# Attention scores of the second pair of heads: three float32r products of split operands in place of one float32 product

## The chip, the cores and the metric

The kernel runs on one core of one Trainium2 chip. The metric is the device time of one execution in microseconds; three runs gave 1058.92, 1059.16 and 1059.59, median 1059.16 us. A core has TensorE (PE; its weight loads are shown as PEld), VectorE (DVE), ScalarE (ACT), GpSimd (POOL) and SyncE (SP), which here issues nearly all DMA transfers. PSUM, the memory that TensorE writes, has eight banks of 2 KB a partition; SBUF holds the rest of the on-chip data in 128 partitions.

## The reference

Inputs are q, k and v of shape 8 x 12 x 448 x 64 (batches, heads, positions, width of a head), two weight matrices of 768 x 2048 and 2048 x 768, and two scalars. All is float32.

```python
scores = scale * np.matmul(q, k.transpose(0, 1, 3, 2)) - np.log(S)
attn = 1.0 / (1.0 + np.exp(-scores))
attn_out = np.matmul(attn, v)
x = attn_out.transpose(0, 2, 1, 3).reshape(B * S, H * D)     # 3584 x 768
h = x @ w_in
g = s * np.maximum(h, 0.0) ** 2 + b
out = g @ w_out
```

The sigmoid takes the place of a softmax, so there is no row sum: each score goes through scale, bias and sigmoid by itself, and the result multiplies v. Then comes a feed-forward block over all 3584 tokens.

## The kernel before

The program is laid out by hand: the order in which instructions are written is the order of each engine's queue, and a tile of memory that is used again makes its next writer wait for the last readers.

**Attention stage.** 24 steps ("quads", line 333), three to a batch, each of four heads. The four heads are two pairs: index i is the pair, index j the head within it. The two heads of a pair lie in partitions 0 to 63 and 64 to 127 of the tiles `q` and `k` (`half`, line 332). `scores` (L357) goes over the pairs and over three blocks c of 128 keys; for each it computes two float32 products of 64 contraction rows, one for each head, into a PSUM tile of two banks (L365), and ACT turns both at once into weights by a sigmoid (L354). The last 64 keys of all four heads go together in 64x64 tiles (`scores_last`, L372, products L377); this is written for step n+1 behind the attention products of step n. `attn_v` (L383, products L388) and `attn_v_last` (L394, L397) multiply by v and add up in one PSUM tile `pav` of two banks. `store_x` (L402) copies it out on DVE, one copy for each pair (L405), and stores both (L406).

PSUM in this stage: three tiles of two banks for scores (`ps_qk`) and one for `pav` (`ps_av`); the third block of keys of the first pair also uses the latter (L362), so it has to wait until `pav` of the step before has been copied.

**What runs beside it.** The weights come as 64-bit floating-point numbers. Meanwhile DVE and ACT turn them into float32 (`convert`, L186: L193, then L197 on ACT, then L199 to L209), build sums of blocks of them for a fast matrix product of the feed-forward stages (`sums`, L220, from the table `SUMS`), split everything into two float32r parts (`hi` is the value cast to float32r on ACT, `lo` the rest, a subtraction on DVE) and store it in DRAM (`wd`). The table `ROWS` says which stored row holds which sum.

**Order.** `plan` maps a step and an engine to jobs with ranks. In a step the loop at L519 writes: DVE jobs; the scores with their sigmoids; ACT jobs; the loads of step n+2 (L346) and further SP jobs; stores held back; attention products; the last scores of step n+1; the copies and stores of `pav`. A step that converts a tile (`piece`) runs L193 on DVE and L197 on ACT, and the other four operations on DVE one step later.

**Behind the attention.** `ffn1` and `ffn2` work off the first 512 tokens with the split weights while the other sums are finished (L489, L668). Tokens are loaded into `x0l` at step 20, cast to `x0h` in step 22 and subtracted in step 23. Then two rounds of three blocks of 512 tokens follow (L924 and L1051). All feed-forward products take three float32r products for one of float32: with parts (weight, data) hi·hi, hi·lo and lo·hi, in the order of `PARTS` (L39).

Of the kernel before, what the change touches and what calls it, by code (L numbers as in the profile page):

```python
# [11 lines left out]
F32 = mybir.dt.float32  # L12
# [29 lines left out]
LATE, LATE_AT, LATE_FOR = 2, 2, 5  # L42
SUMS_AT = (2, 5, 8, 11, 14, 17, 20, 22)
ROLL = 7

# [8 lines left out]
    ),  # L54
    (
# [4 lines left out]
    ),  # L60
)

ROWS = (
    ("p", "q", "r", "u", "v", "w", "x", "y", "z", "d", "00", "10", "20", "01", "11"),
    ("p", "q", "r", "u", "v", "w", "x", "y", "z", "d", "01", "02", "10", "11", "12"),
)

FIRST = {
# [16 lines left out]
def sigmoid_attention_relu2_ffn(  # L85
    ctx: ExitStack,
    tc: tile.TileContext,
    q: bass.AP,
    k: bass.AP,
    v: bass.AP,  # L90
    w_in: bass.AP,
    w_out: bass.AP,
# [2 lines left out]
    out: bass.AP,  # L95
):
    nc = tc.nc
    B, NQ, P, _, S = q.shape
    D = v.shape[5]
    NF, _, DM = w_in.shape  # L100
    NCC = DM // P
# [12 lines left out]
    def pool(stack, name, bufs, side=None, space=None):  # L114
        kw = dict(side=side) if side else {}
        if space is not None:
            kw["space"] = space
        return stack.enter_context(
            tc.tile_pool(name=name, bufs=bufs, reuse_waits="tile", **kw)
        )  # L120
# [44 lines left out]
    def f32(ap):  # L165
        return ap.bitcast(F32)
# [4 lines left out]
    def sub(o, x, y):  # L171
# [1 line left out]


    order = [f + h * NP for f in range(NP) for h in range(2)]
    wf = {
        l: {
            f: (wfp_last if f % NP == NP - 1 else wfp).tile(
                [P, 3, KW], F32, tag=f"wf_{l}_{f}", name=f"wf_{l}_{f}"
            )  # L180
            for f in order
        }
        for l in (1, 0)
    }

    def convert(l, f, st):  # L186

# [32 lines left out]
    def sums(l, f, tl):  # L220

        raw, ts = {}, []

        def val(n):
            return raw[n] if n in raw else block(l, f, n)

        def make(g):
            t = tl.tile([P, 3, 2, KW], F32R, name=f"t_{l}_{f}_{g}")
            ts.append(t)
            k = 0  # L230
            for n, x, sign, y in SUMS[l][g]:
                if n == "t":
                    raw[n] = f32(t[:, 0, 0])
                else:
                    raw[n] = f32(t[:, k, 1])
                    k += 1
                op(raw[n], val(x), sign, val(y))

        def hi(g):
            nc.scalar.copy(ts[g][:, :, 0], f32(ts[g][:, :, 1]))  # L240

        def lo(g):
            t = ts[g]
            sub(t[:, :, 1], f32(t[:, :, 1]), f32(t[:, :, 0]))

            def store():
                nc.sync.dma_start(
                    wd[l][f // 2][:, 3 * g : 3 * g + 3, f % 2],
                    f32(t).rearrange("p k h c -> p k (h c)"),
                )  # L250
                tl.free(t)

            if l:
                stores.append(store)
            else:
                store()

        make(0)
        make(1)
        yield  # L260
        hi(0)
        hi(1)
        yield
        make(2)
        lo(0)
        lo(1)
        yield
        hi(2)
        yield
        lo(2)  # L270
        yield
# [50 lines left out]

    at = ExitStack()
    ap_ = pool(at, "ap", 8)
    xo = pool(at, "xo", 3)
    ldv = pool(at, "ldv", 3)
    qk = ExitStack()
    ld = pool(qk, "ld", 2)
    ps_qk = pool(qk, "ps_qk", 3, space=PSUM)
    ps_av = pool(at, "ps_av", 1, space=PSUM, side="right")  # L330

    half = (slice(0, D), slice(D, P))
# [1 line left out]
    NL = len(quads)  # L334

    def load(b, t, first=False):
        qt = ld.tile([P, 2, S], F32, tag="q", name=f"q_{b}_{t}")
        kt = ld.tile([P, 2, S], F32, tag="k", name=f"k_{b}_{t}")
        vt = ldv.tile([P, 7, 2, D], F32, tag="v", name=f"v_{b}_{t}")
        if first:  # L340
            nc.sync.dma_start(kt[:, 0, :P], k[b, t][:, 0, :P])
            nc.scalar.dma_start(qt[:, 0], q[b, t][:, 0])
            nc.sync.dma_start(kt[:, 0, P:], k[b, t][:, 0, P:])
            nc.scalar.dma_start(qt[:, 1], q[b, t][:, 1])
            nc.sync.dma_start(kt[:, 1], k[b, t][:, 1])
        else:  # L346
            nc.sync.dma_start(kt, k[b, t])
            nc.sync.dma_start(qt, q[b, t])
        nc.sync.dma_start(vt, v[b, t])
        return qt, kt, vt  # L350

    def sigmoid(psc, name):
        a = ap_.tile([P, 2, S], F32, tag="a", name=f"a_{name}")
# [1 line left out]
        return a  # L355

    def scores(b, t, i, ld_):  # L357
        qt, kt, _ = ld_
        a = []
        for c in range(3):  # L360

            pl, tag = (ps_av, "pav") if i == 0 and c == 2 else (ps_qk, "psc")  # L362
            psc = pl.tile([P, 2, 512], F32, tag=tag, name=f"psc_{b}_{t}_{i}_{c}")
            for j, r in enumerate(half):
                nc.tensor.matmul(  # L365
                    psc[:, j, :S], kt[r, i, c * P : (c + 1) * P], qt[r, i, :],
                    start=True, stop=True,
                )
            a.append(sigmoid(psc, f"{b}_{t}_{i}_{c}"))
        return a  # L370

    def scores_last(b, t, ld_):  # L372
        qt, kt, _ = ld_
        psc = ps_qk.tile([P, 2, 512], F32, tag="psc", name=f"psc_{b}_{t}_l")
        for j, r in enumerate(half):
            for i in range(2):
                nc.tensor.matmul(  # L377
                    psc[half[i], j, :S], kt[r, i, 3 * P :], qt[r, i, :],
                    start=True, stop=True,
                )  # L380
        return sigmoid(psc, f"{b}_{t}_l")

    def attn_v(b, t, ld_, a):  # L383
        pav = ps_av.tile([P, 2, 512], F32, tag="pav", name=f"pav_{b}_{t}")
        for i in range(2):
            for c in range(3):
                for j, r in enumerate(half):
                    nc.tensor.matmul(  # L388
                        pav[r, i, :S], ld_[2][:, 3 * i + c, j, :], a[i][c][:, j, :],
                        start=c == 0, stop=False,  # L390
                    )
        return pav

    def attn_v_last(ld_, a, pav):  # L394
        for i in range(2):
            for j, r in enumerate(half):
                nc.tensor.matmul(  # L397
                    pav[r, i, :S], ld_[2][half[i], 6, j, :], a[half[i], j, :],
                    start=False, stop=True,
                )  # L400

    def store_x(b, t, pav):  # L402
        for i in range(2):
            o = xo.tile([P, S], F32, tag="xo", name=f"xo_{b}_{t}_{i}")
            nc.vector.tensor_copy(o, pav[:, i, :S])  # L405
            nc.sync.dma_start(x_dram[b][:, 2 * t + i], o)  # L406

    loaded = {0: load(*quads[0], first=True)}
    nc.scalar.activation(e_bias, nls, AF.Sigmoid)
    nc.vector.memset(e_bias, -896.0 * 2.0**23)  # L410

# [9 lines left out]
    def at_step(n, part, rank, fn):  # L421
        jobs = plan.setdefault((n, part), [])
        jobs.append((rank, len(jobs), fn))
# [48 lines left out]

    ticks(-1, "SP")
    loaded[1] = load(*quads[1])
    nc.sync.dma_start(s_sb, s)
    nc.sync.dma_start(b_sb, b_)

# [24 lines left out]
    def first_hi(h):  # L502
        hi = cx.tile([P, HC, TB], F32R, name=f"x0h_{h}")
        nc.scalar.copy(hi, f32(x0[h]))
        x0[h] = (hi, x0[h])
# [5 lines left out]
    w1 = []  # L511
    for h in range(2):
        at_step(NL - 4, "SP", 1, lambda h=h: first_tokens(h))
        at_step(NL - 2, "ACT", 7, lambda h=h: first_hi(h))
        at_step(NL - 1, "DVE", 0, lambda h=h: first_lo(h))
    at_step(NL - 2, "ACT", 8, lambda: w1.append(base_hi(0, 0)))
    at_step(NL - 1, "DVE", 1, lambda: base(0, 0, w1[0]))

    for n, (b, t) in enumerate(quads):  # L519
        ticks(n, "DVE")  # L520
        a = [scores(b, t, i, loaded[n]) for i in range(2)]
        if n == 0:
            al = scores_last(b, t, loaded[0])
        ticks(n, "ACT")
        if n + 2 < NL:
            loaded[n + 2] = load(*quads[n + 2])
        ticks(n, "SP")
        for fn in stores:
            fn()
        stores.clear()  # L530
        if n == NL - 1:
            qk.close()
            ps_h = pool(blk_ps, "ps_h", 2, space=PSUM)
        pav = attn_v(b, t, loaded[n], a)
        attn_v_last(loaded[n], al, pav)
        if n + 1 < NL:
            al = scores_last(*quads[n + 1], loaded[n + 1])
        store_x(b, t, pav)
    ticks(NL, "DVE")
    for fn in stores:  # L540
        fn()
# [7 lines left out]
    gp = pool(blk, "gp", 3)  # L549
    ps_o = pool(blk_ps, "ps_o", 1, space=PSUM)  # L550
    cx.more(pool(blk, "t2", 1), 4, "t")
    assert not plan

    threes = [tuple(1 + 3 * n + i for i in range(3)) for n in range((NT - 1) // 3)]
# [562 lines left out]
```

## Time and profile before

| | |
|---|---|
| median of three runs | 1059.16 us |
| profiled execution, its own time | 1059.26 us |
| its span | 1057.1 us |
| TensorE busy | 1052.8 us |
| DVE busy | 794.0 us |
| ACT busy | 586.1 us |
| DMA queue of SP, share of 16 engines' time over the span | 78.1% |
| float32 score products, L365 (576 instructions) | 115.8 us busy |
| float32 products with v, L388 (576 instructions) | 113.5 us busy |
| first feed-forward product starts | 270.25 us |

Busy times of PE are unions of instructions that overlap, and the end of a product is modelled; the length of one instruction is its latency and not the distance to the next. The distance is read from starts. Lines such as L169, L172 and L354 are helpers: all additions, subtractions or sigmoids show under one line, and the tile names tell them apart. The profile's chain of waits goes back from the last instruction, at each step to what released it or to the one before it on its engine.

### The profile page before, as it was taken

What the parts mean: (1) busy time and instruction counts of PE and PEld (TensorE: products, weight loads), DVE (VectorE), ACT (ScalarE), POOL (GpSimd) and SP (SyncE); (2) the same over time, 40 slices, a digit from 0 to 9 for tenths busy, and PEclk for the clock granted to TensorE, in tenths of its full rate; (3) what the DMA queues carried; (4) which work ended last, traced back from release to release, by engine and by line L of the source; (5) the groups of instructions that cost most, each with busy time, mean ns of one, the idle gap of its engine ahead of it and who ended that gap; (6) DMA issues with size and microseconds to landing.
All of it is one profiled execution on the core that took longest, in us unless ns stands there. A gap on an engine that the chain in (4) does not pass through costs nothing.

```text
span 1057.1 us, 13342 instructions
## 1 busy us (share of the span) xinstructions
PE 1052.8 (100%) x5011; PEld 756.1 (72%) x5011; DVE 794.0 (75%) x915; ACT 586.1 (55%) x638; POOL 0.2 (0%) x4
## 2 busy tenths in 40 slices
PE   9999999999999999999999999999999999999998
PEld 4433434333788888888888888888888888888887
DVE  3787877778788866455888799697455789888777
ACT  6777778778776766354436443344444336443432
POOL 0000000000000000000000000000000000000000
PEclk9999999999999999999999999999999999999999
DMA  8899999997899999866666667797666666677673
GB/s 310 282 337 372 333 332 333 335 391 272 332 382 343 371 368 408 275 195 197 191 190 196 198 232 229 252 334 270 196 198 188 194 196 193 190 232 221 208 233 118
DMA packets 105614, 280.84 MB, mean 266 GB/s; under 512 B 10576, under 2 KB 26832, under 8 KB 105552
## 3 DMA queue, kind: packets, MB, share of 16 engines
q1 hardware_dynamic: 105264, 279.55, 78.1%
q8 instruction: 40, 0.66, 0.2%
q10 hardware_dynamic: 288, 0.46, 0.1%
q14 instruction: 22, 0.18, 0.1%
HBM read 195.04 MB, written 84.93 MB: 265 GB/s over the span
## 4 chain that ended last, share of the span: by engine, by line
PE 99%; ACT 0%; DVE 0%; issue 0%
PE o L1051 31%; PE h L924 31%; PE pav L388 11%; PE psc L365 10%; PE ph L489 6%; PE po L668 6%; PE pav L397 2%; PE psc_l L377 2%; ACT a L354 0%; PE idle L414 0%; DVE C_t L172 0%; DVE zero L156 0%; DVE nls L157 0%
## 5 line engine op out<-in xcount | busy, mean ns | idle before, releaser
L924 PE MATMUL h<-s_0h,wu 128*128 128x512 f32 x480 | 148.0, 389 | 0.0
L924 PE MATMUL h<-s_1h,wu 128*128 128x512 f32 x480 | 147.9, 389 | 0.0
L354 ACT ACTIVATE a<-psc,nls 128x896 f32<-128x896 f32 x144 | 132.2, 1019 | 2.5 <-PE psc L365 2.4
L365 PE MATMUL psc<-q,k 64*128 64x448 f32 x576 | 115.8, 548 | 0.0
L388 PE MATMUL pav<-a,v 128*64 128x448 f32 x576 | 113.5, 543 | 0.0
L924 PEld LDWEIGHTS h<-s_0h,wu 128*128 128x128 f32 x480 | 90.1, 188 | 18.8
L924 PEld LDWEIGHTS h<-s_1h,wu 128*128 128x128 f32 x480 | 90.1, 188 | 18.6
L797 ACT COPY G<-h 128x1024 f32<-128x1024 f32 x48 | 48.9, 1019 | 93.1 <-PE h L924 61.9
L365 PEld LDWEIGHTS psc<-q,k 64*128 64x128 f32 x576 | 53.6, 188 | 61.6 <-issue 37.4
L169 DVE TENSOR_TENSOR G<-G,h 128x1024 f32<-128x1024 f32 x40 | 48.8, 1220 | 61.7 <-PE h L924 61.7
L763 ACT ACTIVATE G<-G,b_sb,s_sb 128x1024 f32<-128x1024 f32 x48 | 59.9, 1248 | 62.8 <-DVE G L760 62.1
L924 PE MATMUL h<-s_0l,wu 128*128 128x512 f32 x240 | 93.4, 389 | 0.0
L924 PE MATMUL h<-s_1l,wu 128*128 128x512 f32 x240 | 93.4, 389 | 0.0
L388 PEld LDWEIGHTS pav<-a,v 128*64 128x64 f32 x576 | 39.2, 137 | 71.4 <-issue 63.0
L1051 PE MATMUL o<-g_3h,wu 128*128 128x512 f32 (+1 forms) x244 | 78.9, 385 | 0.0
L1051 PE MATMUL o<-g_0h,wu 128*128 128x512 f32 x240 | 78.7, 389 | 0.0
L1051 PE MATMUL o<-g_1h,wu 128*128 128x512 f32 x240 | 78.7, 389 | 0.0
L1051 PE MATMUL o<-g_2h,wu 128*128 128x512 f32 x240 | 78.7, 389 | 0.0
L405 DVE COPY xo<-pav 128x448 f32<-128x448 f32 x48 | 27.7, 620 | 55.9 <-PE pav L397 55.9
L668 PE MATMUL po<-g,w 128*128 128x512 f32 x288 | 67.7, 389 | 0.0
L668 PEld LDWEIGHTS po<-g,w 128*128 128x128 f32 x288 | 54.1, 188 | 11.2
L489 PE MATMUL ph<-x0h,w 128*128 128x512 f32 x192 | 61.6, 390 | 0.0
(126 smaller groups left out, 1823.0 us busy)
## 6 DMA issues: line engine op xcount, KB each, us to landing
wu<-wd SPq DMA_DIRECT2D x240, 512.0 KB, 3.5
wd<-t SPq DMA_DIRECT2D x48, 768.0 KB, 9.1
st<-w_out SPq DMA_DIRECT2D x16, 768.0 KB, 8.5
st<-w_in SPq DMA_DIRECT2D x16, 768.0 KB, 8.4
wd<-w SPq DMA_DIRECT2D x16, 768.0 KB, 4.9
v<-v_t SPq DMA_DIRECT2D x24, 448.0 KB, 6.2
xd<-xo SPq DMA_DIRECT2D x48, 224.0 KB, 6.4
k<-k_t SPq DMA_DIRECT2D x23, 448.0 KB, 4.5
```

Of the source, the lines that this page charges most:

```text
L169: nc.vector.tensor_tensor(o, x, y, op=ALU.add)
L354: nc.scalar.activation(a, psc[:, :, :S], AF.Sigmoid, bias=nls, scale=SCALE)
L365: nc.tensor.matmul(psc[:, j, :S], kt[r, i, c * P : (c + 1) * P], qt[r, i, :], start=True, stop=True,)
L377: nc.tensor.matmul(psc[half[i], j, :S], kt[r, i, 3 * P :], qt[r, i, :], start=True, stop=True,)
L388: nc.tensor.matmul(pav[r, i, :S], ld_[2][:, 3 * i + c, j, :], a[i][c][:, j, :], start=c == 0, stop=False,)
L405: nc.vector.tensor_copy(o, pav[:, i, :S])
L489: nc.tensor.matmul(ph, w[:, k, wi, kc * P : (kc + 1) * P], x0[h][xi][:, cc, :], start=m == 0, stop=m == 3 * NCC - 1,)
L668: nc.tensor.matmul(pos[e], w[:, k, wi, kc * P : (kc + 1) * P], g[:, gi, :], start=first and i == 0, stop=last and i == 2,)
L763: nc.scalar.activation(x, x, AF.Identity, bias=b_sb, scale=s_sb)
L797: nc.scalar.copy(g(m, h), bk)
L924: nc.tensor.matmul(bk[:, j], wt[:, j, wi, c * P : (c + 1) * P], opd[i][xi][:, c, :], start=i == ch[0] and m == 0, stop=m == 3 * KC - 1, sk ...
L1051: nc.tensor.matmul(o, wt[:, f, wi, e * P : (e + 1) * P], g[gi][:, f, tk], start=(end or i == ch[0] and p == 0) and f == 0 and m == 0, stop ...
```

## The change

For steps 1 to 23, the scores of the second pair (i = 1) against the first 384 keys are no longer float32 products of q and k. q and k of that pair are split into two float32r parts, and each product becomes three: k hi with q hi, k hi with q lo, k lo with q hi, added up in PSUM. Step 0, the first pair and the last 64 keys keep float32.

- q and k now come from DRAM in one array `qk` and one tile [128, pair, q or k, 448]; a step's load is one transfer in place of two.
- `parts_hi` (ACT) casts 448 columns of q and 384 of k of the next step's second pair in one instruction, behind the sigmoids of this step and ahead of ACT's jobs. `parts_lo` (DVE) subtracts as many, behind DVE's jobs and ahead of the copy of `pav`.
- Within a block of keys the order is: first product for both heads, second for both, third for both.
- `pav` is copied by one instruction and stored by one transfer. The load of v for step n+2 is issued behind that store; it was issued with q and k.
- Buffers: `xo` 3 of one pair to 2 of two pairs, `ldv` 3 to 2, and a pool `hl` for the parts. The two weight tiles that are converted last lie in a pool that is opened after the attention.
- In the second weight's `SUMS`, q and r, and y and x, are each made by one operation on two blocks; `ROWS` follows.
- The cast of the second half of the first tokens moves from ACT's jobs of step 22 to those of step 23, its subtraction to a new place in step 23, behind the attention products and ahead of the copy of `pav`.

```diff
+TWO = range(1, 24)
...
-        (("p", "00", -1, "10"), ("q", "02", -1, "p"), ("r", "01", -1, "p")),
+        (("p", "00", -1, "10"), ("rq", "01", -1, "p")),
...
-        (("x", "12", -1, "q"), ("y", "11", -1, "r"), ("z", "00", -1, "01")),
+        (("yx", "11", -1, "rq"), ("z", "00", -1, "01")),
...
+                if len(n) == 2:
+                    raw[n] = f32(t[:, k : k + 2, 1])
+                    raw[n[0]], raw[n[1]] = f32(t[:, k, 1]), f32(t[:, k + 1, 1])
+                    two = raw[y] if len(y) == 2 else raw[y].unsqueeze(1).to_broadcast([P, 2, KW])
+                    h, b0 = int(x[0]), int(x[1])
+                    op(raw[n], wf[l][f + h * NP][:, b0 : b0 + 2], sign, two)
+                    k += 2
+                    continue
...
-    xo = pool(at, "xo", 3)
-    ldv = pool(at, "ldv", 3)
-    qk = ExitStack()
-    ld = pool(qk, "ld", 2)
-    ps_qk = pool(qk, "ps_qk", 3, space=PSUM)
+    xo = pool(at, "xo", 2)
+    ldv = pool(at, "ldv", 2)
+    qkx = ExitStack()
+    ld = pool(qkx, "ld", 2)
+    hl = pool(qkx, "hl", 1)
+    ps_qk = pool(qkx, "ps_qk", 3, space=PSUM)
...
-        qt = ld.tile([P, 2, S], F32, tag="q", name=f"q_{b}_{t}")
-        kt = ld.tile([P, 2, S], F32, tag="k", name=f"k_{b}_{t}")
+        x = ld.tile([P, 2, 2, S], F32, tag="qk", name=f"qk_{b}_{t}")
...
-            nc.sync.dma_start(kt, k[b, t])
-            nc.sync.dma_start(qt, q[b, t])
+            nc.sync.dma_start(x, qk[b, t])
+        return [x]
+
+    def load_v(b, t, ld_):
+        vt = ldv.tile([P, 7, 2, D], F32, tag="v", name=f"v_{b}_{t}")
         nc.sync.dma_start(vt, v[b, t])
-        return qt, kt, vt
+        ld_.append(vt)
+
+    NX = S + 3 * P
+
+    def flat(t):
+        return t.rearrange("p x s -> p (x s)")[:, :NX]
+
+    def parts_hi(b, t, ld_):
+        hi, lo = (hl.tile([P, 2, S], F32R, tag=h, name=f"qk{h}_{b}_{t}") for h in "hl")
+        nc.scalar.copy(flat(hi), flat(ld_[0][:, 1]))
+        ld_.append((hi, lo))
+
+    def parts_lo(ld_):
+        hi, lo = ld_[-1]
+        sub(flat(lo), flat(ld_[0][:, 1]), f32(flat(hi)))
...
+            if two:
+                for m, (wi, xi) in enumerate(PARTS):
+                    for j, r in enumerate(half):
+                        nc.tensor.matmul(
+                            psc[:, j, :S], two[wi][r, 1, cols], two[xi][r, 0, :],
+                            start=m == 0, stop=m == 2,
+                        )
+            else:
...
-        for i in range(2):
-            o = xo.tile([P, S], F32, tag="xo", name=f"xo_{b}_{t}_{i}")
-            nc.vector.tensor_copy(o, pav[:, i, :S])
-            nc.sync.dma_start(x_dram[b][:, 2 * t + i], o)
+        o = xo.tile([P, 2, S], F32, tag="xo", name=f"xo_{b}_{t}")
+        nc.vector.tensor_copy(o, pav[:, :, :S])
+        nc.sync.dma_start(x_dram[b][:, 2 * t : 2 * t + 2], o)
...
-        at_step(NL - 2, "ACT", 7, lambda h=h: first_hi(h))
-        at_step(NL - 1, "DVE", 0, lambda h=h: first_lo(h))
+        at_step(NL - 2 + h, "ACT", 7, lambda h=h: first_hi(h))
+    at_step(NL - 1, "DVE", 0, lambda: first_lo(0))
+    at_step(NL - 1, "END", 0, lambda: first_lo(1))
...
+        if n + 1 in TWO:
+            parts_hi(*quads[n + 1], loaded[n + 1])
         ticks(n, "ACT")
...
         if n + 1 < NL:
             al = scores_last(*quads[n + 1], loaded[n + 1])
+        if n + 1 in TWO:
+            parts_lo(loaded[n + 1])
+        ticks(n, "END")
         store_x(b, t, pav)
+        if n + 2 < NL:
+            load_v(*quads[n + 2], loaded[n + 2])
```

More of the change, by code (lines that the diff above doesn't have):

```diff
@@ L64 @@
     ("p", "q", "r", "u", "v", "w", "x", "y", "z", "d", "00", "10", "20", "01", "11"),
-    ("p", "q", "r", "u", "v", "w", "x", "y", "z", "d", "01", "02", "10", "11", "12"),
+    ("p", "r", "q", "u", "v", "w", "y", "x", "z", "d", "01", "02", "10", "11", "12"),
 )
@@ L87, in sigmoid_attention_relu2_ffn @@
     tc: tile.TileContext,
-    q: bass.AP,
-    k: bass.AP,
+    qk: bass.AP,
     v: bass.AP,
@@ L97, in sigmoid_attention_relu2_ffn @@
     nc = tc.nc
-    B, NQ, P, _, S = q.shape
+    B, NQ, P, _, _, S = qk.shape
     D = v.shape[5]
@@ L175, in sigmoid_attention_relu2_ffn, with wf_tile @@
     order = [f + h * NP for f in range(NP) for h in range(2)]
[L176 to L184, printed above, removed]
+    wf = {1: {}, 0: {}}
+    def wf_tile(l, f, pl):
+        wf[l][f] = pl.tile([P, 3, KW], F32, tag=f"wf_{l}_{f}", name=f"wf_{l}_{f}")
+    for f in order:
+        wf_tile(1, f, wfp_last if f % NP == NP - 1 else wfp)
+        if f % NP < NP - 1:
+            wf_tile(0, f, wfp)
     def convert(l, f, st):
@@ L336, in load @@
     def load(b, t, first=False):
-        qt = ld.tile([P, 2, S], F32, tag="q", name=f"q_{b}_{t}")
-        kt = ld.tile([P, 2, S], F32, tag="k", name=f"k_{b}_{t}")
-        vt = ldv.tile([P, 7, 2, D], F32, tag="v", name=f"v_{b}_{t}")
[L340 to L346, printed above, removed]
-            nc.sync.dma_start(kt, k[b, t])
-            nc.sync.dma_start(qt, q[b, t])
-        nc.sync.dma_start(vt, v[b, t])
-        return qt, kt, vt
+        x = ld.tile([P, 2, 2, S], F32, tag="qk", name=f"qk_{b}_{t}")
+        if first:
+            nc.sync.dma_start(x[:, 0, 1, :P], qk[b, t][:, 0, 1, :P])
+            nc.scalar.dma_start(x[:, 0, 0], qk[b, t][:, 0, 0])
+            nc.sync.dma_start(x[:, 0, 1, P:], qk[b, t][:, 0, 1, P:])
+            nc.scalar.dma_start(x[:, 1, 0], qk[b, t][:, 1, 0])
+            nc.sync.dma_start(x[:, 1, 1], qk[b, t][:, 1, 1])
+        else:
+            nc.sync.dma_start(x, qk[b, t])
+        return [x]
+    def load_v(b, t, ld_):
+        vt = ldv.tile([P, 7, 2, D], F32, tag="v", name=f"v_{b}_{t}")
+        nc.sync.dma_start(vt, v[b, t])
+        ld_.append(vt)
[9 more added lines that the diff above has]
+        sub(flat(lo), flat(ld_[0][:, 1]), f32(flat(hi)))
     def sigmoid(psc, name):
@@ L357, in scores @@
     def scores(b, t, i, ld_):
-        qt, kt, _ = ld_
+        x = ld_[0]
+        two = ld_.pop() if i and len(ld_) > 2 else None
         a = []
@@ L363, in scores @@
             psc = pl.tile([P, 2, 512], F32, tag=tag, name=f"psc_{b}_{t}_{i}_{c}")
[L364 to L368, printed above, removed]
+            cols = slice(c * P, (c + 1) * P)
+            if two:
[5 more added lines that the diff above has]
+                        )
+            else:
+                for j, r in enumerate(half):
+                    nc.tensor.matmul(
+                        psc[:, j, :S], x[r, i, 1, cols], x[r, i, 0, :],
+                        start=True, stop=True,
+                    )
             a.append(sigmoid(psc, f"{b}_{t}_{i}_{c}"))
@@ L372, in scores_last @@
     def scores_last(b, t, ld_):
-        qt, kt, _ = ld_
+        x = ld_[0]
         psc = ps_qk.tile([P, 2, 512], F32, tag="psc", name=f"psc_{b}_{t}_l")
@@ L377, in scores_last @@
                 nc.tensor.matmul(
-                    psc[half[i], j, :S], kt[r, i, 3 * P :], qt[r, i, :],
+                    psc[half[i], j, :S], x[r, i, 1, 3 * P :], x[r, i, 0, :],
                     start=True, stop=True,
@@ L388, in attn_v @@
                     nc.tensor.matmul(
-                        pav[r, i, :S], ld_[2][:, 3 * i + c, j, :], a[i][c][:, j, :],
+                        pav[r, i, :S], ld_[1][:, 3 * i + c, j, :], a[i][c][:, j, :],
                         start=c == 0, stop=False,
@@ L397, in attn_v_last @@
                 nc.tensor.matmul(
-                    pav[r, i, :S], ld_[2][half[i], 6, j, :], a[half[i], j, :],
+                    pav[r, i, :S], ld_[1][half[i], 6, j, :], a[half[i], j, :],
                     start=False, stop=True,
@@ L402, in store_x @@
     def store_x(b, t, pav):
-        for i in range(2):
-            o = xo.tile([P, S], F32, tag="xo", name=f"xo_{b}_{t}_{i}")
-            nc.vector.tensor_copy(o, pav[:, i, :S])
-            nc.sync.dma_start(x_dram[b][:, 2 * t + i], o)
+        o = xo.tile([P, 2, S], F32, tag="xo", name=f"xo_{b}_{t}")
+        nc.vector.tensor_copy(o, pav[:, :, :S])
+        nc.sync.dma_start(x_dram[b][:, 2 * t : 2 * t + 2], o)
     loaded = {0: load(*quads[0], first=True)}
+    load_v(*quads[0], loaded[0])
     nc.scalar.activation(e_bias, nls, AF.Sigmoid)
@@ L474, in sigmoid_attention_relu2_ffn @@
     loaded[1] = load(*quads[1])
+    load_v(*quads[1], loaded[1])
     nc.sync.dma_start(s_sb, s)
@@ L531, in sigmoid_attention_relu2_ffn @@
         if n == NL - 1:
-            qk.close()
+            qkx.close()
             ps_h = pool(blk_ps, "ps_h", 2, space=PSUM)
@@ L551, in sigmoid_attention_relu2_ffn @@
     cx.more(pool(blk, "t2", 1), 4, "t")
+    wfp_late = pool(blk, "wfp_late", 1)
+    for _, f in late:
+        wf_tile(0, f, wfp_late)
     assert not plan
@@ L1098 @@
     arrays = {
-        "q_t": rows(q),
-        "k_t": rows(k),
+        "qk_t": np.ascontiguousarray(np.stack((rows(q), rows(k)), axis=4)),
         "v_t": v_t,
```

## The prediction

> **What bounds the kernel now.** I read the page's busy shares and its chain of waits first, to see which engine sets the end; then the chain in order of time over the attention stage; then TensorE's weight loads, for the length of one product; last the ACT and DVE queues of single steps, for the room that the new work finds.
>
> ```profile
> span 1057.1 us, 13342 instructions
> PE 1052.8 (100%) x5011; PEld 756.1 (72%) x5011; DVE 794.0 (75%) x915; ACT 586.1 (55%) x638; POOL 0.2 (0%) x4
> ...
> PE 99%; ACT 0%; DVE 0%; issue 0%
> ```
>
> TensorE is busy all the time, and 99% of the chain is its own work. So a microsecond taken out of its stream is a microsecond off the end, as long as nothing else comes late.
>
> The chain in order of time (start, length, what), first one ordinary step of four heads, then the last two:
>
> ```profile
> 16.65 4.71 PE psc L365 x24
> 21.36 4.66 PE pav L388 x24
> 26.02 0.91 PE pav L397 x8
> 26.94 0.75 PE psc_l L377 x8
> ...
> 248.41 5.04 PE psc L365 x24
> ...
> 259.77 4.91 PE psc L365 x24
> ```
>
> A step is 4.71 + 4.66 + 0.91 + 0.75 = 11.03 us, with no gap. Only in the last two steps do the scores take 5.04 and 4.91: something other than TensorE is late there, by 0.33 and 0.20.
>
> **The scores, float32.** The 12 float32 products of a step's scores show as 24 instructions, two for each. Their weight loads:
>
> ```profile
> 126.94 0.30 PEld L365 LDWEIGHTS psc<-q,k 64*128 64x128 f32 x4 [0.70 <-PE pav L397]
> 127.42 0.19 PEld L365 LDWEIGHTS psc<-q,k 64*128 64x128 f32 x2 [0.18 <-issue]
> 127.80 0.19 PEld L365 LDWEIGHTS psc<-q,k 64*128 64x128 f32 x2 [0.18 <-issue]
> ```
>
> Two loads of 64 rows finish in 0.19 us together, the length of one: the two heads of a pair (rows 0 to 63 and 64 to 127) run side by side. Such a couple comes every 0.37 to 0.38 us (127.42, 127.80), and a pair of heads needs two couples for each block of 128 keys: 0.747 us (six of them are 4.48; the other 0.23 of the 4.71 is the entry from the 64x64 tiles). That is 1.67 ns for each of 448 columns, four times the 0.417 that the next rows give for float32r.
>
> **The scores, float32r.** The trace has no float32r product of 64 rows. It has them with 128 rows, 720 in each of the last four stretches, the third of which is shown, and at the very end some of 256 columns:
>
> ```profile
> 727.44 163.20 PE h L924 x720
> ...
> L924 PEld LDWEIGHTS h<-s_0h,wu 128*128 128x128 f32 x480 | 90.1, 188 | 18.8
> ...
> 1052.43 0.28 PE L1051 MATMUL o<-g_3l,wu 128*128 128x256 f32 x1
> 1052.55 0.40 PE L1051 MATMUL o<-g_3h,wu 128*128 128x256 f32 x2
> 1052.79 0.28 PE L1051 MATMUL o<-g_3l,wu 128*128 128x256 f32 x1
> ```
>
> 163.20 / 720 = 227 ns for 512 columns, one instruction each. At the end three of 256 columns start within 1052.79 - 1052.43 = 0.36, so 120 ns each. From these two points a column costs (227 - 120)/256 = 0.417 ns and a product 13 ns besides: 200 ns for 448 columns, if the two halves go side by side as the float32 ones do; without the 13 it would be 187. A 128-column weight load every 120 ns was no obstacle, although one takes 188. By the Trainium skill, "TensorE: Matmul & The Clock Gate", Back-to-back issue gap, N/2.4 + 2.5, the 448 columns would take 189 ns and the gain would be 12.4 us rather than 10.1. The 227 ns of this trace against its 216 for 512 columns decide for the longer.
>
> A block of keys of the second pair falls from 747 to 3 x 200 = 600 ns: 0.147 us less, three blocks in a step, 0.44; 23 steps (the first keeps float32), **10.1 us less**. Bounds for the product: 187 ns gives 12.9 us; two halves one after the other, 400 ns, gives a loss (below). The change of type inside the scores adds an entry between 0 (psc_l after pav_l, same tile shape: 0.75, no entry) and 0.23 (psc above): 0 to 5.3 us over 23 steps. I take 0, since the shape stays 64x128.
>
> **What ACT and DVE get.** Each of 23 steps adds a cast of 832 elements a row (448 of q, 384 of k) on ACT and a subtraction of as many on DVE. Two copies of 448 out of PSUM become one of 896; the merged sums make one operation of 512 elements out of two of 256, twice in every third step.
>
> ```profile
> L240 ACT CAST t<-t 128x768 fp32r<-128x768 f32 x48 | 38.3, 832 | 1.8 <-DVE t L169 1.5 <-DVE t L172 0.3
> L581 ACT CAST s_0h<-a 128x1024 fp32r<-128x1024 f32 x9 | 9.5, 1058 | 5.4 <-DVE a L172 4.1 <-DVE a L169 1.3
> L172 DVE TENSOR_TENSOR t<-t 128x768 fp32r<-128x768 f32 x48 | 44.4, 953 | 0.7 <-ACT t L240 0.7
> L172 DVE TENSOR_TENSOR s_0l<-a,s_0h 128x1024 fp32r<-128x1024 f32 x9 | 11.0, 1223 | 3.9 <-ACT s_0h L581 3.7 <-DMA a<-xd 0.3
> L405 DVE COPY xo<-pav 128x448 f32<-128x448 f32 x48 | 27.7, 620 | 55.9 <-PE pav L397 55.9
> ```
>
> Between the rows for 768 and 1024: the cast 832 + 226/4 = 0.89 us, the subtraction 953 + 270/4 = 1.02 us. One copy of 896 for two of 448 is worth under 0.1 us, by the pair that the next rows give as 1.16 (one, by DVE's slope of 270 ns for 256 elements, 0.62 + 0.47 = 1.09); the sums save as little. So ACT +0.9, DVE +0.9 in a step that gets 0.44 shorter. The steps with least room:
>
> ```profile
> 71.83:82.87 11.04, 11.04 (x67) 4.39 (x66) 8.86 (x16) 9.51 (x11) 0.00 (x0) 1.00 0.89 292
> 82.87:93.90 11.03, 11.03 (x66) 4.38 (x66) 9.80 (x14) 7.43 (x8) 0.00 (x0) 1.00 1.01 394
> 237.36:248.39 11.03, 11.03 (x68) 4.38 (x66) 10.82 (x16) 6.89 (x8) 0.00 (x0) 1.00 1.03 365
> sum 264.84, PE 264.79 PEld 104.28 DVE 199.40 ACT 206.29 POOL 0.00; mean PE 11.03 PEld 4.35 DVE 8.31 ACT 8.60 POOL 0.00
> ...
> 72.89 5.50 ACT L354 ACTIVATE a<-psc,nls 128x896 f32<-128x896 f32 x6
> 79.67 1.77 ACT L197 ACTIVATE wf<-wf,e_bias 128x768 int32<-128x768 int32 x2 [1.28 <-DVE wf L193]
> 82.94 1.01 ACT L354 ACTIVATE a_l<-psc_l,nls 128x896 f32<-128x896 f32 x1 [0.25 <-PE psc_l L377]
> 93.22 1.16 DVE L405 COPY xo<-pav 128x448 f32<-128x448 f32 x2 [1.02 <-PE pav L397]
> 248.00 0.94 ACT L197 ACTIVATE wf<-wf,e_bias 128x768 int32<-128x768 int32 x1 [4.07 <-DVE wf L193]
> 249.57 1.00 ACT L354 ACTIVATE a_l<-psc_l,nls 128x896 f32<-128x896 f32 x1
> ```
>
> (First rows: the window, its length, then busy time of PE, weight loads, DVE, ACT and POOL, the granted clock, DMA share and GB/s; the sum is over all 24 steps.) ACT: behind the new cast stand the step's weight conversion and casts, then the sigmoid of psc_l, then those of the next scores. In the step from 71.83 the six sigmoids end at 78.4 and ACT stands idle for 1.28 and for 0.25 us: the cast's 0.9 goes into the 1.28 and hides. The step's end comes 0.44 earlier against 0.25 of idle time, so psc_l's sigmoid is 0.2 late. It may be: the last block of keys is the first that needs a score buffer whose sigmoid would be the latest, and it starts 0.23 + 3 x 0.747 + 2 x 0.6 = 3.67 us into the scores, while the sigmoids that it needs end three times 0.92 (5.50 / 6) and the tail of one after psc_l's starts, near 2.95; room, 0.7 us. Without the 1.28 the cost would be 0.4 us in such a step. DVE: in the step from 82.87 it stood idle for 1.02 us ahead of the copy; the subtraction stands there now, and with the shorter step the copy comes 0.4 to 0.5 late. Behind it waits the third block of the next scores, which takes the buffer of pav 0.75 + 0.23 + 1.49 = 2.47 us after pav is done; 1.09 of copying leaves 1.38. Hidden; without that cover 0.4 a step.
>
> Not hidden are the last two. From 237.36 DVE has 10.82 of 11.03 us, the conversion on ACT waits for it until 248.00, and psc_l's sigmoid starts 1.16 into the step. With a step 0.44 shorter it starts 1.5 to 1.6 into it, against 0.7 of room: a stall of 0.8 to 0.9 where 0.33 was. That is some 0.6 more. In the next step one of the two token casts leaves ACT and the new cast comes, behind a late start: an estimate of the same 0.6 on its 0.20. **1.2 us back** in all. The token cast and subtraction that move (the second half of the tokens) are wanted first by the eleventh of the 18 products behind the last step, 2.3 us into them; if they came later, that lateness would be added once.
>
> **Transfers.** Per step k and q come in one issue instead of two, the stores of pav in one instead of two, and v moves behind that store on SP's queue.
>
> ```profile
> v<-v_t SPq DMA_DIRECT2D x24, 448.0 KB, 6.2
> q<-q_t SPq DMA_DIRECT2D x23, 448.0 KB, 5.3
> ```
>
> v is issued some 5 us later than now, but is used a step and 3.6 us after that, 14 us for a landing of 6.2. q and k can start when the first pair's scores are done, 2 us earlier, and the cast needs them 14 us on, for 5.3. No cost; without that cover the cast would hold ACT and with it all sigmoids. The bytes stay, in a step 4% shorter. The DMA shares of the three steps above are 0.89, 1.01 and 1.03: in steps like the last two, transfers will queue longer. With the 8 us to spare for v and q I add nothing to the sum; for the range I allow that the stage shortens only half as far in a third of the steps, 2 to 3 us. The late weight tiles (placed in memory freed by the attention) are used well after that.
>
> **The sum:** 1059.26 (the profiled execution; its span is 1057.1, with 2.2 around it) - 10.1 + 1.2 = 1050.4. That execution lies 0.1 over the median of the three runs, 1059.16: I predict **1050.3**.
>
> **The rivals.** (a) *Halves in turn.* If a float32r product takes the whole array, the couple costs 400 ns, a block 1200 instead of 747: 0.453 x 69 = 31.3 us, **1090**. It would decide from 249 ns a couple (747/3) on. For it: every float32r product in the trace has 128 rows, and those of 64 rows are all float32 by the code. Against: the loads above show that two halves are independent for 4-byte data. 9%.
>
> (b) *Loads in the open.* If a half's next weights could not be loaded behind its own running product, a couple would cost 188 + 187 = 375, a block 1125: 0.378 x 69 = 26 us, **1085**. Against it: L924 loads for 188 ns and yet has a product every 227. 3%. The Trainium skill states it so, in "TensorE: Matmul & The Clock Gate", Part 3, The mechanism: a load overlaps products in flight only where the row group differs. By that rule this change would lose; the L924 rows do not agree with it. A milder form: the two loads of a couple take turns at 107 to 120 ns (four loads in 0.30 above, two of them 0.11 later), so a couple takes 214 to 240: a gain of 1.9 to 7.2, less 1.2, **1053 to 1059**. The 0.19 for two speaks against it; 8%.
>
> (c) *ACT or DVE becomes the bound.* The mean of ACT, 8.6 us, and of DVE, 8.3, become 9.5 and 9.2 of 10.6, and each waits for the other within a step (the cast for the last sigmoid, the subtraction for the cast, the copy behind it). If every step loses 0.2 to 0.4 so, 5 to 9 us go: **1054 to 1059**, 12%. If the subtraction comes late in each step by over 1.38 us, the scores wait for pav's buffer, and from 0.44 of waiting a step the change is a loss; at 0.7, 6 us: **1065**, 6%. The 55.9 / 23 = 2.43 us that DVE now waits on average ahead of the copy speak against it.
>
> (d) *Transfers set the pace.* A stage at full DMA share that gives back the 3 us above ends at 1053, within the main case's range and counted there.
>
> **How the numbers follow.** Main case 62% (1046 to 1054.5: 187 ns at the low end; entries of 0.1 us, 2.3, and the 3 of the transfers, not both in full, at the upper); (a) 9, (b) 3 and 8, (c) 12 and 6. Of the milder cases about 7 points lie within 0.2% (2.1 us) of before, about what this kernel's runs can tell from no change. Faster 0.75, same 0.07, slower 0.18. The range, 1046 to 1062, leaves out (a), (b)'s hard form, half of (c)'s loss, and a little below.
>
> **What would show it.** Scores of 4.71 turned 4.27 in the chain, with six couples of loads at 0.37 and nine at 0.20; a step of 10.6. Couples over 0.25 apart show (a) or (b). A copy on DVE with no wait for pav ahead of it, and scores longer than 4.3 in ordinary steps, would show (c); waits of the cast for q and k, (d). Wrong I am if float32r in 64 rows costs more than 249 ns a couple.

## The result, and the profile after

The changed kernel takes 1051.02 us (median of four runs, 1050.09 to 1051.34); the kernel before, in four runs, 1059.04. The ratio is 0.9922, interval 0.9905 to 0.9939: 8.0 us faster. The profiled execution took 1051.34 us. Three executions of 3.8 to 6.2 ms among those of this document (one each of the kernel before, of the layout alone and of the first run with an operation of step 21 moved) count in none of its ratios.

The page's first rows and its chain by engine, after:

```profile
span 1049.5 us, 13591 instructions
PE 1044.9 (100%) x5149; PEld 769.9 (73%) x5149; DVE 813.2 (77%) x898; ACT 601.8 (57%) x661; POOL 0.2 (0%) x4
...
PE 99%; DVE 0%; issue 0%
```

TensorE still sets the end. DVE has 19 us more to do than before and ACT 16, and neither shows up in the chain with a full percent. The chain in order of time, after: the start of step 1, one ordinary step, then the end of the attention stage.

```profile
17.40 2.46 PE psc L401 x12
...
81.20 2.46 PE psc L401 x12
83.66 1.85 PE psc L395 x16
...
230.07 2.46 PE psc L401 x12
...
245.88 4.73 PE pav L424 x24
...
254.74 1.86 PE psc L395 x18
...
262.17 4.76 PE ph L526 x20
...
266.95 3.92 PE ph L526 x16
```

L401 is the first pair in float32, L395 the second in float32r. Six steps take 81.20 - 17.40 = 63.80 us, one 10.63 instead of 11.03, and all of it comes from the scores, 2.46 + 1.85 = 4.31 instead of 4.71. The attention ends at 262.17 instead of 270.25. The scores of step 22 start 10.63 after 230.07, at 240.70, and its products with v at 245.88: 5.18 us, a stall of 0.87. In step 23 (1.86) there is none. The first feed-forward products have a new one: 36 of them take 266.95 + 3.92 - 262.17 = 8.70 us, where the chain of before has 8.39:

```profile
270.25 8.39 PE ph L489 x36
```

The float32r couples' weight loads after, two of the nine of a step:

```profile
116.01 0.20 PEld L395 LDWEIGHTS psc<-qkl,qkh 64*128 64x128 f32 x2
116.21 0.19 PEld L395 LDWEIGHTS psc<-qkh,qkl 64*128 64x128 f32 x2
```

Two loads together, 0.20 us behind the couple before, with no idle time between: the heads run side by side, in half the 0.37 of float32's couples.

The new work on ACT and DVE and the merged copy, as groups of the profile after:

```profile
L371 ACT CAST qkh<-qk 128x832 fp32r<-128x832 f32 x23 | 21.0, 913 | 0.9 <-DMA qk<-qk_t 0.9
L173 DVE TENSOR_TENSOR qkl<-qk,qkh 128x832 fp32r<-128x832 f32 x23 | 23.5, 1021 | 4.5 <-ACT qkh L371 4.5
L440 DVE COPY xo<-pav 128x896 f32<-128x896 f32 x24 | 26.2, 1090 | 22.2 <-PE pav L433 22.2
```

913, 1021 and 1090 ns, where the prediction had 0.89, 1.02 and 1.09. What DVE waits for `pav` ahead of the copy fell from 55.9 us to 22.2: the subtraction went into that wait. The cast waited for q and k once, in step 0.

One part of the difference between the two profiles does not come from the scores of steps 1 to 23. The weight loads of step 0, the same float32 products in both kernels, before and then after:

```profile
4.84 0.34 PEld L365 LDWEIGHTS psc<-q,k 64*128 64x128 f32 x2 [0.41 <-issue]
5.37 0.19 PEld L365 LDWEIGHTS psc<-q,k 64*128 64x128 f32 x2 [0.19 <-issue]
```

```profile
4.84 0.34 PEld L401 LDWEIGHTS psc<-qk 64*128 64x128 f32 x2 [0.41 <-DMA qk<-qk_t]
5.59 0.34 PEld L401 LDWEIGHTS psc<-qk 64*128 64x128 f32 x2 [0.41 <-issue]
6.33 0.34 PEld L401 LDWEIGHTS psc<-qk 64*128 64x128 f32 x2 [0.41 <-issue]
```

Couples 0.75 apart are at half the pace of 0.37: TensorE runs at half speed until about 5 us in the one execution and until past 6.3 in the other (the traces record the full clock as granted from 5.1 and from 6.9 us on), and step 1 starts 0.75 us later (17.40 instead of 16.65). Among the traces used below the full clock comes between 3.7 and 7.0 us, in kernels with the same layout too (3.7 with the parts made once, 6.6 with the layout alone), and step 1 starts between 16.6 and 17.5, without any order in the kernels. The Trainium skill ("TensorE: Matmul & The Clock Gate", Part 1) says that the clock rises after a window of activity that runs freely, so that the point differs from run to run; that agrees. Steps are therefore compared from the start of step 1 on.

### The profile page after: what moved, and what is told of

Same layout as the page of the kernel before. It is cut to its first block, busy times and chain, and to the rows that moved or that the text cites. A ratio compares the mean times of both kernels' runs of the same rounds, so it can differ in the third digit from the quotient of the medians.

```text
span 1049.5 us, 13591 instructions
## 1 busy us (share of the span) xinstructions
PE 1044.9 (100%) x5149; PEld 769.9 (73%) x5149; DVE 813.2 (77%) x898; ACT 601.8 (57%) x661; POOL 0.2 (0%) x4
## 4 chain that ended last, share of the span: by engine, by line
PE 99%; DVE 0%; issue 0%
PE o L1099 31%; PE h L972 31%; PE pav L424 11%; PE ph L526 6%; PE po L716 6%; PE psc L401 6%; PE psc L395 4%; PE pav L433 2%; PE psc_l L413 2%; PE idle L450 0%; DVE xo L440 0%; DVE qkl L173 0%; DVE wf L194 0%; DVE C_t L173 0%; DVE zero L157 0%
## 5 line engine op out<-in xcount | busy, mean ns | idle before, releaser
L401 PE MATMUL psc<-qk 64*128 64x448 f32 x300 | 64.6, 564 | 0.1
L401 PEld LDWEIGHTS psc<-qk 64*128 64x128 f32 x300 | 27.5, 191 | 36.5 <-issue 16.6
L1099 PEld LDWEIGHTS o<-g_3h,wu 128*128 128x128 f32 x244 | 45.6, 188 | 9.2
```

The costliest lines, as they stand in the source:

```text
L401: nc.tensor.matmul(psc[:, j, :S], x[r, i, 1, cols], x[r, i, 0, :], start=True, stop=True,)
L1099: nc.tensor.matmul(o, wt[:, f, wi, e * P : (e + 1) * P], g[gi][:, f, tk], start=(end or i == ch[0] and p == 0) and f == 0 and m == 0, stop ...
```

## The experiments

**Only the layout.** The changed kernel with `TWO = ()`.

```diff
-TWO = range(1, 24)
+TWO = ()
```

> The changed kernel with no step in TWO: one transfer of q and k, one copy and store of pav, v behind the store, merged sums, the moved token cast; all scores float32. Theory: the layout alone gives nothing, since TensorE sets each step: steps of 11.03 us and 1058.5 to 1059.8 us, as before. Rival: part of the 8 us comes from fewer transfers and copies: 1057 us or less, with the 5.04 and 4.91 us of the last two steps' scores gone back to 4.71.

Measured: 1058.86 us, ratio to before 0.9993 (0.9983 to 1.0003). The end of the stage in the chain of waits:

```profile
249.00 4.90 PE psc L401 x24
...
260.23 4.71 PE psc L401 x24
...
270.51 8.43 PE ph L526 x36
```

No difference that the runs can tell. In the trace the last step has lost its stall (4.71 where 4.91 was), and the step before has 0.19 instead of 0.33: 0.34 us from the layout. The last step's stall went with the token cast that was moved. ACT in front of the last step, before and then with the layout alone:

```profile
257.27 2.89 ACT L504 CAST x0h<-x0l 128x1536 fp32r<-128x1536 f32 x2
260.75 1.05 ACT L354 ACTIVATE a_l<-psc_l,nls 128x896 f32<-128x896 f32 x1
```

```profile
257.73 1.52 ACT L541 CAST x0h<-x0l 128x1536 fp32r<-128x1536 f32 x1
260.29 1.01 ACT L380 ACTIVATE a_l<-psc_l,nls 128x896 f32<-128x896 f32 x1 [0.32 <-PE psc_l L413]
```

With one cast in place of two, psc_l's sigmoid starts 0.06 us into the step instead of 0.98. Another 0.3 to 0.4 us lies around the span: 1059.1 - 1057.3 = 1.8 us here, 1.84 in the changed kernel, 2.16 before, and the other runs of these kernels lie as close to these values. It comes with the layout; which part of it does this, no run shows. The rest of the 8 us is not from fewer transfers or copies.

**The parts made, but not used.** The casts and subtractions run, the scores stay float32.

```diff
         two = ld_.pop() if i and len(ld_) > 2 else None
+        two = None
```

> The parts are cast and subtracted as in the changed kernel, but the scores take float32 q and k in every step. Theory: the work on ACT and DVE is hidden in all steps but the last three, which get 0.2 to 0.8 us longer in all: 1059 to 1060 us, ordinary steps of 11.03 us. Rival: ACT and DVE cost something in each step, 0.2 to 0.4 us, that the products then have to win back: 1063 to 1068 us.

Measured: 1059.05 us, ratio 0.9997 (0.9988 to 1.0007). Steps of 11.03 us throughout. The stall of step 22 is 0.18 and step 23 has none, as with the layout alone, so the 0.2 to 0.8 us expected for the last steps did not come either. With a step of that length the work on ACT and DVE costs nothing.

**The products without the work.** The parts are made once and used 23 times, so the second pair's scores are those of step 1 in all later steps.

```diff
-TWO = range(1, 24)
+TWO = range(1, 2)
...
-        two = ld_.pop() if i and len(ld_) > 2 else None
+        two = parts[0] if i and parts and (b, t) != quads[0] else None
```

> The parts are made once, for step 1, and the second pair of every step from 1 on multiplies these same parts (so its scores are those of step 1): the float32r products without the work on ACT and DVE. Theory: 0.40 us off each of 23 steps, 9.25 us, less some 0.4 us of stall at step 21, where DVE had 10.82 us of work before: 1049.8 to 1050.8 us, steps of 10.63 us. Rival, that the parts cost time in ordinary steps: steps under 10.55 us and 1048 us or less.

Measured: 1049.90 us, ratio 0.9908 (0.9891 to 0.9926). Chain of waits of this kernel:

```profile
16.61 2.46 PE psc L404 x12
...
239.88 2.46 PE psc L404 x12
...
245.06 4.73 PE pav L427 x24
...
261.30 8.46 PE ph L529 x36
```

From the start of step 1 to the first feed-forward product it takes 261.30 - 16.61 = 244.69 us; the changed kernel, 262.17 - 17.40 = 244.77. So all the casts and subtractions together cost 0.08 us in the stage, and 0.24 in the first feed-forward products behind it (8.70 against 8.46); most of the rest between the two times is the clock of step 0 (16.61 for 17.40). Step 22 has its stall here too, 245.06 - 239.88 = 5.18 us of scores, so 0.87 and not the 0.4 expected, with no subtraction anywhere near. What ACT does in front of it:

```profile
239.74 0.94 ACT L198 ACTIVATE wf<-wf,e_bias 128x768 int32<-128x768 int32 x1 [3.94 <-DVE wf L194]
241.31 1.00 ACT L383 ACTIVATE a_l<-psc_l,nls 128x896 f32<-128x896 f32 x1
```

ACT waits 3.94 us for the first operation of the conversion, which stands at the end of DVE's 10 us of work, and psc_l's sigmoid starts 241.31 - 239.88 = 1.43 us into the step. That is the prediction's account of step 22.

**That wait taken away.** In step 21 the operation (L194 in the changed kernel) moves ahead of the second of the two older conversions.

```diff
-        at_step(n, "DVE", 9, lambda: (g.append(convert(l, f, st[0])), next(g[0])))
+        at_step(n, "DVE", 4 if n == 21 else 9, lambda: (g.append(convert(l, f, st[0])), next(g[0])))
...
-        at_step(n + 1, "DVE", 3, last)
+        at_step(n + 1, "DVE", 5 if n == 20 and plan.get((n + 1, "DVE"))
+                and any(r == 3 for r, _, _ in plan[n + 1, "DVE"]) else 3, last)
```

> The changed kernel with one DVE instruction moved: in step 21 the first operation of that step's conversion (L194) stands ahead of the second of the two older conversions instead of behind it, 3.4 us earlier, so that ACT's part of the conversion no longer waits for it. Theory: the stall of 0.87 us in the scores of step 22 comes from ACT waiting for this instruction, and falls to 0.1 or less; 0.7 to 0.85 us off, near 1050.2 us, and the scores of step 22 in 4.3 to 4.4 us. Rival: it comes from the copy of pav, late behind the subtraction: the stall stays at 0.8 us, and so does the time.

Measured: 1049.5 to 1050.2 us, ratio 0.9908 (0.9892 to 0.9925). The kernel was run once more, for its trace:

> The changed kernel with L194 of step 21 moved 3.4 us earlier on DVE, as in the run before, for its trace. Theory: ACT no longer waits in step 21, and what is left of the 0.87 us in the scores of step 22 is the copy of pav, late behind DVE's 11.7 us of work: 0.1 to 0.5 us; near 1050.0 us. Rival: ACT's wait returns elsewhere in step 22 or 23, and the steps from 21 on take as long as in the changed kernel.

Measured: 1050.26 us, ratio 0.9915 (0.9898 to 0.9931). This second run in order of time:

```profile
240.68 1.78 PE L401 MATMUL psc<-qk 64*128 64x448 f32 x8
240.82 1.01 ACT L380 ACTIVATE a_l<-psc_l,nls 128x896 f32<-128x896 f32 x1 [1.81 <-PE psc_l L413]
242.62 1.02 PE L401 MATMUL psc<-qk 64*128 64x448 f32 x4 [0.17 <-DVE xo L440]
...
245.39 4.73 PE L424 MATMUL pav<-a,v 128*64 128x448 f32 x24
```

psc_l's sigmoid is on time and now itself waits for TensorE. The scores of step 22 take 245.39 - 240.68 = 4.71 us: the stall is 0.40 and not 0.1 or less, and its cause is the other one, the third block waiting for the copy of `pav` behind the subtraction. The two stalls lay over each other: ACT's gives 0.87 (the parts made once), DVE's alone 0.40. The chain of waits behind the stage:

```profile
261.67 8.43 PE ph L526 x36
```

The stretch from step 1 to the first feed-forward product is 0.55 us shorter in the traces (261.67 - 17.45 = 244.22), and the first feed-forward products another 0.27 (8.43 for 8.70), 0.8 in all. The times point the same way (1049.5 to 1050.2 and 1050.0 to 1050.6 for 1050.1 to 1051.3), but their ranges touch.

**DVE's cover doubled away.** The subtraction is written twice in each step.

```diff
         sub(flat(lo), flat(ld_[0][:, 1]), f32(flat(hi)))
+        sub(flat(lo), flat(ld_[0][:, 1]), f32(flat(hi)))
```

> The changed kernel with the subtraction of the parts written twice a step (the second writes the same values): 1.02 us more on DVE in each of 23 steps. In the changed kernel the copy of pav still waits 0.3 to 1.6 us for pav in most steps. Theory: doubling eats that cover, and a step is lost only where the copy comes over 1.4 us late: 0 to 3 us in all, 1051 to 1054 us. Rival: the cover was used up by the first subtraction, and the second costs most of its 1.02 us in each step: 1065 us or more.

Measured, in one run: 1052.48 us. From step 1 to the first feed-forward product 263.91 - 17.14 = 246.77 us, 2.0 more than the changed kernel. The chain of waits around one of the steps that lose:

```profile
92.27 1.09 DVE xo L441
...
93.41 1.02 PE psc L402 x4
```

The third block of scores (93.41) waits for the copy, and the chain goes back through DVE. This happens behind the four fullest steps (7, 13, 19, 21) and nowhere else: 23.5 us of DVE work cost 2.0.

**The heads of a pair in turn.** The three products of one head are issued together, then those of the other.

```diff
-                for m, (wi, xi) in enumerate(PARTS):
-                    for j, r in enumerate(half):
+                for j, r in enumerate(half):
+                    for m, (wi, xi) in enumerate(PARTS):
```

> The three products of one head are issued together and then those of the other; the same products and parts. Theory: float32r products run side by side only while neighbours in TensorE's queue lie in different rows, so a block of keys takes 1.20 us instead of 0.61 (some 0.4 us less if the third product of the first head runs beside the first of the second): 69 blocks, 13 to 41 us more, 1064 to 1092 us. Rival: TensorE pulls the other head's products forward, and the time stays at 1051 us.

Measured, in one run: 1051.26 us, the time of the changed kernel. The second pair's 18 products of step 1, in the chain of waits of this kernel:

```profile
19.62 1.85 PE psc L395 x18
```

That is the changed kernel's 1.85. The theory fell: neighbours in the queue need not lie in different rows. TensorE ran the other head's products beside the first's though they stand three places behind. (The places are those of the kernel's text; the trace shows starts, not places in the queue.)

**Nine apart.** All nine products of the first head, then the nine of the second.

```diff
+            for j, r in enumerate(half):
+                for c in range(3):
+                    for m, (wi, xi) in enumerate(PARTS):
+                        nc.tensor.matmul(
+                            ps3[c][:, j, :S], two[wi][r, 1, c * P : (c + 1) * P], two[xi][r, 0, :],
+                            start=m == 0, stop=m == 2,
+                        )
+            return [sigmoid(ps3[c], f"{b}_{t}_{i}_{c}") for c in range(3)]
```

> The changed kernel with the second pair's products in another order: all nine of the first head (three blocks of keys), then all nine of the second. Theory after the run with the heads in turn: TensorE lets products on the other 64 rows run ahead in its queue; if it reaches nine products ahead, the scores stay at 4.31 us and the time near 1051 us; if it reaches only a few, the second pair takes up to 3.6 us instead of 1.85 and a step up to 1.8 us more: up to 1092 us.

Measured, in one run: 1075.61 us. The second pair takes 2.97 us instead of 1.85 (chain of waits), and its weight loads show why:

```profile
102.14 2.97 PE psc L392 x18
```

```profile
102.79 0.18 PEld L392 LDWEIGHTS psc<-qkh,qkl 64*128 64x128 f32 x1
102.99 0.18 PEld L392 LDWEIGHTS psc<-qkh 64*128 64x128 f32 x2
103.10 0.28 PEld L392 LDWEIGHTS psc<-qkl,qkh 64*128 64x128 f32 x2
103.31 0.27 PEld L392 LDWEIGHTS psc<-qkh,qkl 64*128 64x128 f32 x2
103.51 0.18 PEld L392 LDWEIGHTS psc<-qkh 64*128 64x128 f32 x1
```

The loads come one by one, 0.20 apart; only in the middle do three come in twos. A single product of 64 rows takes 0.20 us, as long as two side by side, and TensorE here reaches three products ahead and no further: 18 products in 15 places of 0.20. A step is 2.97 - 1.85 = 1.12 us longer than in the changed kernel; 23 of them are 25.8, less the 0.87 of step 22, which is gone in the longer steps: 24.9, and 24.6 was measured. So this order alone makes the change a loss, by the mechanism of rival (a), heads one after the other, and at 1.12 of the 1.8 us a step that it would cost in full (400 instead of 200 ns for each of nine couples).

**Both pairs where there is room.** With the edit of step 21, and the parts of both pairs in nine steps ahead of which DVE has room; one buffer less for the sigmoids and one for the copies.

```diff
+BOTH = (3, 4, 6, 9, 10, 12, 15, 16, 18)
...
-        nc.scalar.copy(flat(hi), flat(ld_[0][:, 1]))
+        if both:
+            nc.scalar.copy(flat2(hi), flat2(ld_[0]))
+        else:
+            nc.scalar.copy(flat(hi[:, 1]), flat(ld_[0][:, 1]))
...
-    ap_ = pool(at, "ap", 8)
-    xo = pool(at, "xo", 2)
+    ap_ = pool(at, "ap", 7)
+    xo = pool(at, "xo", 1)
```

> As the run before, and in nine steps (3, 4, 6, 9, 10, 12, 15, 16, 18, ahead of which DVE has room) the parts are made of both pairs of heads, in one cast and one subtraction of 1728 elements, and all scores of full blocks take three float32r products; one buffer less for the sigmoids' results and one for the copies of pav make the room. Theory: 0.40 us less in each of nine steps, since the longer cast (0.8 us more) and subtraction (0.95 us more) still hide: 3.6 us off, 1046.5 to 1047.5 us. Rival: ACT becomes the bound in these steps, which then gain nothing: 1050 us or more.

Measured: 1046.46 us, ratio to before 0.9876 (0.9860 to 0.9893): faster than both kernels. A step with all blocks in float32r, in the chain of waits of this kernel:

```profile
69.75 3.86 PE psc L406 x36
```

3.86 against 4.31, 0.45 less where 0.40 was expected; from step 1 on the stage takes 258.46 - 17.28 = 241.18 us, 3.0 less than the 244.22 with the edit of step 21 alone, of the 3.6 expected. Two small costs make the difference: behind such scores the products with v start 0.02 us later and take 4.73 instead of 4.66, so a step falls by 0.35, and step 13, behind one of these steps, takes 0.20 longer than an ordinary one:

```profile
142.74 2.46 PE psc L412 x12
145.19 1.97 PE psc L406 x17
```

(1.97 for 1.85, and 4.73 behind it.)

**Both pairs in fourteen steps.**

```diff
-BOTH = (3, 4, 6, 9, 10, 12, 15, 16, 18)
+BOTH = (1, 2, 3, 4, 5, 6, 9, 10, 11, 12, 15, 16, 17, 18)
```

> Parts of both pairs in fourteen steps instead of nine: 1, 2, 5, 11 and 17 as well. Ahead of steps 5, 11 and 17 DVE has 9.2 us of work besides (before the change's own 0.9), so with the longer subtraction some 11.1 us in a step of 10.23. Theory: 0.40 us less for each of steps 1 and 2; for the other three the copy of pav comes about 1 us late, just inside the room that the next scores leave, so 0 to 0.40 each: 1044.5 to 1046 us. Rival: DVE is over its room there, the lateness runs on into the steps behind, and it ends at 1046.5 us or more.

Measured: 1046.91 us, ratio 0.9884 (0.9869 to 0.9898); no better. The rival was right: steps 5, 11 and 17 take 10.8 us, where 10.28 was hoped for and 10.63 is the ordinary step, and steps 7, 13 and 19, two steps behind each, 10.83. Step 1 gains nothing either. Where step 5 begins:

```profile
56.58 1.88 DVE qkl L174
...
58.50 3.77 PE psc L406 x34
```

The first scores of the step wait for the subtraction itself. With the parts of the second pair alone they are wanted 2.46 us into the step, and the copy of `pav` has until the third block; with those of both pairs they are wanted at once, and DVE has no room behind a full step. I had counted the copy's room and not this one.

## Why the prediction was right

The prediction was 1050.3 us, range 1046 to 1062; 1051.02 was measured. Its terms, from the traces:

- **The products.** Forecast 200 ns for a couple, 0.44 us a step, 10.1 us. Measured 1.85 / 9 = 206 ns a couple and 0.40 a step: 23 x 0.402 = 9.25 us. The mechanism, two float32r heads side by side at the price read from the 128-row products, was right; the term was 0.9 us too large, some 4 to 6 ns a couple. The estimate by the rule of the Trainium skill ("TensorE: Matmul & The Clock Gate", Back-to-back issue gap), 189 ns, is further off than the row's 200. No entry shows where the type changes: 2.46 is 0.22 + 3 x 0.747.
- **ACT and DVE hidden in ordinary steps.** Right: 0.08 us in the whole stage by the run that makes the parts once. The room counted ahead of the copy was real too: doubling the subtraction cost 2.0 us, in four steps. (The 2.43 us of waiting ahead of the copy are 55.9 over 23 steps; the 48 copies are those of 24, so 2.33. Nothing hangs on it.)
- **1.2 us back in the last steps.** Half right. In step 22 the stall rose from 0.33 to 0.87, as forecast (0.8 to 0.9) and by the wait that was named, ACT for DVE's conversion (0.87 with no subtraction near it). What was not named is that the copy of `pav` comes late there too, 0.40 by itself. In step 23 it did not rise from 0.20, it went: the step that failed is "the same 0.6 on its 0.20". The token cast that left ACT is worth more (1.4 us, 2.89 - 1.52) than the new cast costs (0.9): psc_l's sigmoid starts 252.73 - 252.28 = 0.45 us into step 23, where before it started 0.98 into it. With the 0.3 of the next term the end of the stage gave back 0.54 - 0.20 + 0.3 = 0.6 us instead of 1.2.
- **The moved tokens.** "That lateness would be added once": 0.3 us in the first feed-forward products (8.70 us for 8.39). DVE after:

```profile
261.80 1.76 DVE L173 TENSOR_TENSOR x0l<-x0l,x0h 128x1536 fp32r<-128x1536 f32 x1 [3.23 <-ACT x0h L541]
```

  The moved subtraction waited 3.23 us for its cast, and the products go on at 266.95, when the first of the weights' two subtractions behind it is done: they waited for weights and not for the tokens themselves. The move alone does not cost this: the layout alone has the same order and takes 8.43. With step 21 mended it is 8.43 too, with the same order and the same casts; there psc_l's sigmoid starts 0.07 us into step 23 (251.86 - 251.79) and not 0.45. So the 0.3 is what was left of ACT's wait in step 21, handed on through the moved cast and subtraction. Whether that lateness would have cost anything without the move, no run shows.
- **Transfers.** No cost showed: the cast waits 0.9 us for q and k in all.

The sum of what was measured: 9.25 - 0.54 + 0.20 - 0.3 = 8.6 us, less 0.75 for the later clock in this one execution, 7.9; the two profiled executions differ by 1059.26 - 1051.34 = 7.9. That these agree to a tenth is chance: the spans differ by only 1057.1 - 1049.5 = 7.6, and 0.3 lies around them (2.16 and 1.84 us), where the prediction kept 2.2; the 0.2 to 0.3 missing inside the span lie mostly behind the chain's last link (2.7 us before, 2.9 after), and no run explains them.

The closeness of the forecast is in part luck too: 0.9 us too much gained on the products and 0.6 too much given back in the last steps pull in opposite directions, and the 0.3 around the span was not foreseen.

Of the rivals, (a) and (b) fell with the couples 0.20 apart; (c) and (d) with the runs above.

## What to carry to other kernels

On a kernel that one engine bounds without a gap, the price of a changed product can be read from a neighbouring shape of the same type, and the rest of the work is to find, step by step, which idle time takes the new instructions on the other engines. Averages did not tell where it would pinch; the step with 10.8 of 11 us did. When two waits end at the same place, taking one away uncovers the other: measure the step, not the wait.

## What the runs showed of the hardware

- A float32r product of 64 rows and 448 columns takes 0.20 us alone and 0.20 beside another on the other 64 rows.
- TensorE runs a product on the other rows beside one that stands three products ahead of it in the kernel's text: with the heads' products three apart nothing is lost (1.85 us for 18), with nine apart only three of nine overlap (2.97 us). The Trainium skill ("TensorE: Matmul & The Clock Gate", Part 3) has products start in strict order; at these distances the runs do not agree with it.
- The time at which TensorE comes to full speed differed by more than a microsecond among executions with the same products in step 0 (5.1 us before, 6.9 after; 3.7 to 7.0 among all the traces), worth 0.75 us between the two profiled executions.
